# Hypermixer after linear attention on one core: k of batch 0 by token, late 64-row transposes, stores whose two tiles take tokens in turn, and another order of work

## The chip, the core and the metric

The kernel runs on one core of one Trainium2 chip. A core has five engines that run their own instruction lists and meet at semaphores: PE (matrix products and transposes, results into the eight PSUM banks), DVE (the vector engine), ACT (the scalar engine), POOL (GpSimd) and SP (SyncE, which here issues every DMA). The 16 DMA engines of the core move the data. The metric is the device time of one execution in microseconds; several executions are made, and their median is compared.

## The reference, cut to what matters

Per batch (8 of them) there are 8 heads, 576 tokens and a head size of 64. First a linear attention with cosine weights by position, then a mixing of tokens by a product of two small projections, and an output projection:

```python
r_q, r_k = relu(q), relu(k)                    # c, s: cos and sin by position
q_p = concat([r_q * c, r_q * s]);  k_p = concat([r_k * c, r_k * s])
kv  = einsum('bhsf,bhsd->bhfd', k_p, v);  z = sum(k_p, axis=2)
x   = einsum('bhsf,bhfd->bhsd', q_p, kv) / (einsum('bhsf,bhf->bhs', q_p, z) + 1e-6)
x   = x, heads side by side: (8, 576, 512)
wq, wk = x @ w_q, x @ w_k                      # 512 -> 64 each
mixed  = (wq @ wk.T / 8) @ x                   # token by token, per batch
out    = relu(mixed) @ w_out                   # 512 -> 512
```

The inputs q, k, v and the output are float32; products run in bf16 with float32 sums.

## The kernel before, in words

The unit of the first half is a group H (0 to 15) of four heads: batch H // 2, half of the heads H % 2. Each group has six loads of 288 KB (`LD.k/q/v.H.j`, two heads each, j is 0 or 1), into rings of four buffers for each of k, q and v (`N_RAW`). Where the prediction speaks of pairs, it means these groups: "pairs 6-15" are H = 6 to 15. A half group is numbered g = 2H + r.

The whole kernel is a text, `ORDER` (line 35), read word by word. `TQ.3@T0` means: step TQ for group 3 on PE, into PSUM bank 0; `@V` is DVE, `@A` ACT, `@G` POOL, `@Y` SP. Each engine executes its own words in the order of the text, without overtaking, and waits where data or a buffer is missing. So a load that waits for its buffer holds every later load and store, as they are all SP's.

The steps of the first half, by group:

- `CV` (line 215) converts v to bf16, `RK` (212) makes relu of k, `DQ` (223) relu of q.
- `VK` (218) multiplies v by the cosine and sine weights, on DVE. `KV` (231) sums k and v over the tokens on PE (36 products), `EK` (241) takes the result out of PSUM.
- `TQ` (245) transposes q on PE: 18 transposes, each on 64 rows of the array. `EQ` (254) multiplies these by the weights, on DVE.
- `NM` (264) gives numerator and denominator of a half group, `RC` (281) adds epsilon to the denominator and inverts it (lines 286 and 287), `XN` (289) multiplies, giving the rows x, on DVE.
- `XT` (300) transposes x on PE. All groups are in `XT_FULL`: ten transposes of 128 by 128. `EX` (317) copies them out of PSUM into xT.

The second half, by batch b:

- `WQK` (328) is the projection of x to q and k at once, with the features on the partitions: 64 rows of wq and 64 of wk. `EW` (337) takes it out. `DW` (341) copies the q rows down to partitions 64 to 127, since the two halves of `MX` need them there.
- `TK` (344) transposes the k rows back so that tokens lie on the partitions; `EWK` (352) takes this out. `KX` (356) sums k times x over the tokens; `EKX` (365) takes it out.
- `MX` (372) multiplies by q, `EMX` (384) applies relu and the scale, into mix.
- `WO` (399) is the output projection of one tile of 128 tokens, four products of 512 columns; `EO` (407) takes it out, `ST` (412) stores a unit of one or two tiles. Units are listed in `UNITS` and `UNITS7` (lines 29, 30); the tiles of batches 2n and 2n+1 lie together, so that nine tiles make two batches.

`LW` and `CW` load and convert the weights. Everything around a word's place in its engine's list, and its PSUM bank, is written out by hand in `ORDER`.

Of the kernel before, what the change touches and what calls it, by code (L numbers as in the profile page):

```python
# [21 lines left out]
EPS = 1.0e-6  # L22
EPS_HI = 9.9837780e-07

N_RAW, N_RK, N_VB, N_VV, N_QD, N_QPT, N_KV = 4, 2, 2, 3, 3, 4, 3
N_XS, N_XT, N_WQK, N_WKJ, N_KX, N_MIX, N_OSB = 3, 2, 2, 2, 2, 2, 8
EPS_PE = False
XT_FULL = (0, 1, 2, 3, 4, 5, 6, 7, 8, 9, 10, 11, 12, 13, 14, 15)
# [7 lines left out]
LD.v.0.1@Y LD.q.1.0@Y LD.v.1.0@Y LD.v.0.0@Y LD.v.1.1@Y LD.k.0.0@Y LD.q.1.1@Y LD.q.0.0@Y  # L36
LD.q.0.1@Y DQ.1.0@A LD.k.0.1@Y CV.0.1@A LD.k.2.1@Y CV.0.0@A LD.k.1.0@Y VK.0.0@V CV.1.1@A
LD.k.1.1@Y VK.0.1@V LD.v.3.0@Y VK.1.1@V DQ.1.1@A LD.q.2.0@Y DQ.0.0@G LD.q.2.1@Y TQ.1@T0 EQ.2@V
RK.0.0@G DQ.0.1@A LD.q.3.0@Y CV.1.0@A LD.v.2.0@Y RK.0.1@G TQ.0@T2 EQ.0@V LD.q.3.1@Y KV.0@T4
EQ.1@V LD.v.2.1@Y EK.0@A EQ.3@V NM.0@T2 LD.k.2.0@Y RK.1.1@A VK.1.0@V NM.1@T4 RK.1.0@A RC.1@V  # L40
LD.k.3.1@Y XN.1@V KV.1@T0 DQ.2.0@G LW.qk@Y RC.0@V EK.1@A CV.3.0@G XN.0@V LD.v.3.1@Y NM.2@T0
RK.2.1@G NM.3@T4 DQ.3.0@A LD.q.5.0@Y RC.2@V XT.0@T2 VK.3.0@V LD.k.3.0@Y CV.2.0@G RC.3@V XN.2@V
DQ.3.1@A LD.q.5.1@Y DQ.2.1@G XN.3@V EX.0@A LD.k.4.0@Y TQ.3@T0 TQ.2@T6 VK.2.0@V XT.1@T4
LD.q.4.0@Y CV.2.1@A EQ.4@V RK.2.0@G EX.1@A LD.v.4.0@Y VK.2.1@V LD.q.4.1@Y CW.qk@G EQ.6@V KV.2@T2
RK.3.1@G EQ.5@V CV.3.1@A LD.v.4.1@Y WQK.0@T4 EK.2@A VK.3.1@V LD.v.5.1@Y NM.5@T2 EW.0@A EQ.7@V
NM.4@T6 LD.k.4.1@Y RK.3.0@G RC.4@V TK.0@T5 DW.0@G RC.5@V LD.k.5.0@Y EWK.0@A KV.3@T0 XN.5@V
DQ.5.1@A KX.0@T5 LD.v.5.0@Y RK.4.0@G EK.3@A XN.4@V EKX.0@A NM.7@T0 DQ.4.0@G LD.k.5.1@Y NM.6@T2
RC.7@V MX.0.2@T4 RC.6@V XT.2@T6 CV.4.0@G LW.o@Y EMX.0.2@A XN.7@V EX.2@A DQ.4.1@G LD.v.6.0@Y
XN.6@V DQ.5.0@G LD.k.6.0@Y TQ.4@T0 CV.4.1@A MX.0.3@T2 EQ.8@V XT.3@T4 CV.5.1@G LD.q.6.0@Y TQ.5@T6
EQ.9@V EX.3@A LD.k.6.1@Y VK.4.0@V MX.0.1@T0 LD.q.6.1@Y RK.4.1@A VK.4.1@V WQK.1@T4 EMX.0.1@A  # L50
LD.v.6.1@Y CV.5.0@G EQ.10@V EMX.0.3@A KV.4@T0 RK.5.0@G LD.q.7.0@Y EW.1@A VK.5.0@V EK.4@A TK.1@T5
RK.5.1@A VK.5.1@V NM.9@T0 MX.0.0@T2 EWK.1@A RC.9@V EMX.0.0@A KV.5@T4 XN.9@V CW.o.0@G LD.v.7.1@Y
KX.1@T3 EK.5@A EQ.11@V CW.o.1@A NM.10@T0 LD.v.7.0@Y CV.6.0@G NM.11@T4 RC.10@V LD.q.8.0@Y
RK.6.0@A WO.0.3@T2 XN.10@V DW.1@G EKX.1@A LD.k.7.1@Y DQ.6.0@A RC.11@V MX.1.0@T0 NM.8@T6 XN.11@V
EO.0.3@A LD.q.7.1@Y RK.6.1@G WO.0.0@T3 EMX.1.0@A VK.6.0@V LD.k.7.0@Y DQ.6.1@A MX.1.1@T4
MX.1.3@T0 RC.8@V WO.0.1@T2 EO.0.0@A CV.6.1@G LD.v.8.0@Y XN.8@V EMX.1.1@A WO.0.2@T3 LD.v.8.1@Y
VK.6.1@V EMX.1.3@A EO.0.1@A MX.1.2@T4 CV.7.1@G LD.q.8.1@Y TQ.6@T0 EO.0.2@A KV.6@T6 EQ.12@V
CV.7.0@G LD.k.8.0@Y EMX.1.2@A XT.5@T2 EQ.13@V EK.6@A LD.q.9.1@Y XT.4@T4 DQ.7.0@A VK.7.0@V
WO.1.4@T7 EX.5@A LD.k.8.1@Y VK.7.1@V NM.12@T0 LD.v.9.1@Y DQ.7.1@G EX.4@A WO.1.0@T6 RC.12@V
LD.q.10.1@Y RK.7.0@G XN.12@V NM.13@T2 EO.1.4@A RK.7.1@G LD.v.9.0@Y TQ.7@T4 EO.1.0@A RC.13@V  # L60
WQK.2@T0 DQ.8.0@G EQ.15@V LD.v.10.0@Y XN.13@V CV.8.1@G KV.7@T6 EW.2@A LD.q.9.0@Y CV.8.0@G
EQ.14@V DQ.8.1@A WO.1.3@T3 LD.q.10.0@Y VK.8.1@V EK.7@A TQ.8@T0 LD.k.9.1@Y EO.1.3@A VK.8.0@V
NM.15@T4 RK.8.0@A WO.1.1@T2 EQ.16@V LD.k.9.0@Y RK.8.1@G DQ.9.1@A EQ.17@V TK.2@T3 NM.14@T6
EO.1.1@A RC.15@V EWK.2@A KV.8@T0 RC.14@V DQ.10.1@G XN.15@V WO.1.2@T3 EK.8@A CV.9.1@G DW.2@A
XN.14@V XT.6@T0 CV.9.0@G EO.1.2@A VK.9.1@V NM.16@T4 LD.v.13.0@Y EX.6@A KX.2@T7 LD.k.10.0@Y
VK.9.0@V LD.k.10.1@Y XT.7@T2 DQ.9.0@G RC.16@V EKX.2@A LD.v.10.1@Y XN.16@V NM.17@T0 EX.7@A
RK.9.1@G LD.v.11.0@Y TQ.9@T6 RC.17@V LD.q.11.0@Y MX.2.2@T4 RK.9.0@G XN.17@V LD.q.11.1@Y
EMX.2.2@A MX.2.0@T2 DQ.10.0@G LD.v.11.1@Y EMX.2.0@A EQ.19@V MX.2.1@T0 ST.1.1@Y KV.9@T4 EMX.2.1@A
EQ.18@V RK.10.0@G LD.k.11.0@Y TQ.10@T2 EK.9@A MX.2.3@T0 LD.k.11.1@Y RK.10.1@G EQ.21@V WQK.3@T6
EMX.2.3@A CV.10.0@G EQ.20@V CV.10.1@A XT.8@T0 EW.3@A VK.10.0@V NM.18@T2 EX.8@A NM.19@T4  # L70
VK.10.1@V TK.3@T7 WO.2.1@T6 DW.3@G RC.19@V RC.18@V DQ.11.1@A XN.19@V WO.2.3@T1 DQ.11.0@G
CV.11.0@A XN.18@V CV.11.1@G EO.2.1@A KV.10@T4 LD.v.15.0@Y VK.11.0@V LD.q.12.0@Y XT.9@T2 EK.10@A
EWK.3@A LD.q.12.1@Y VK.11.1@V NM.20@T4 EX.9@A ST.0.1@Y TQ.11@T6 RK.11.0@G RC.20@V KX.3@T0
LD.q.13.1@Y XN.20@V EO.2.3@A RK.11.1@G LD.v.12.0@Y WQK.4@T2 EQ.22@V EKX.3@A LD.v.12.1@Y
LD.k.12.1@Y EQ.23@V KV.11@T0 EW.4@A LD.v.13.1@Y DQ.12.0@G NM.21@T4 LD.k.12.0@Y EK.11@A MX.3.1@T2
CV.13.0@G TK.4@T7 RC.21@V ST.1.0@Y MX.3.0@T0 EMX.3.1@A WO.2.2@T6 XN.21@V DQ.12.1@G EMX.3.0@A
DW.4@G MX.3.2@T2 EWK.4@A LD.q.13.0@Y TQ.12@T4 EMX.3.2@A NM.23@T0 EQ.24@V KX.4@T7 EO.2.2@A
DQ.13.1@G LD.k.13.1@Y EQ.25@V MX.3.3@T2 EKX.4@A CV.12.0@G ST.0.0@Y WO.2.0@T6 EMX.3.3@A RC.23@V
CV.12.1@A LD.k.13.0@Y VK.12.0@V MX.4.2@T4 NM.22@T2 EO.2.0@A XN.23@V WO.3.0@T7 LD.q.15.1@Y
RK.12.1@G EMX.4.2@A RC.22@V XT.10@T0 LD.v.14.1@Y VK.12.1@V EO.3.0@A WO.3.4@T6 EX.10@A XN.22@V  # L80
LD.q.14.1@Y RK.12.0@G MX.4.1@T4 VK.13.0@V LD.q.14.0@Y KV.12@T2 EO.3.4@A CV.15.0@G LD.k.14.1@Y
XT.11@T0 EMX.4.1@A WO.3.2@T7 EK.12@A DQ.13.0@G EX.11@V LD.v.14.0@Y CV.13.1@A RK.13.1@A NM.25@T2
VK.13.1@V MX.4.0@T0 TQ.13@T4 LD.k.14.0@Y EMX.4.0@A WO.3.1@T6 EQ.26@V EO.3.2@A LD.k.15.0@Y
# [21 lines left out]
def kernel(  # L105
# [28 lines left out]
    def ring(name, shape, dtype, n):  # L134
# [333 lines left out]
    for t in qpt:  # L468
        V.memset(t[:, :, 0, :], 0.0)
# [34 lines left out]
```

## Time and profile before

| quantity | value |
|---|---|
| median of 10 runs | 123.41 us (122.1 to 125.08) |
| the profiled execution | 122.7 us, of which the span is 120.9 |
| mean granted PE clock | 0.958 |
| data by DMA | 39.38 MB, mean 326 GB/s over the span |
| last product of PE ends, last copy by ACT begins | 117.23, 117.26 us |
| loads of 288 KB, from issue to landing | 5.9 to 6.0 us in the median |
| paired stores of 512 KB (15), single stores of 256 KB (6) | 4.7 and 2.5 us to landing |

The page gives for each engine the time that it was busy, then the span in 40 slices of 3 us: a digit is the busy share in tenths, PEclk the granted clock of PE in tenths, DMA the busy share of the DMA engines. A product on PE is recorded with its whole way through the array (a product of 512 columns as 379 ns), while the next one starts long before it is out; how fast PE works when it has no gaps is better read from a run of many. The chain of waits goes back from the last instruction to what released it, and so on to the start; its pieces in order of time tell which engine set the pace in which stretch.

### The profile page before, as it was taken

The page shows a single profiled execution, that of the slowest core. Times are in us where ns is not written, and L with a number is a line of the kernel's source. Part 1 is how long each engine was busy: PE and PEld are TensorE (multiplying, and loading weights), DVE is VectorE, ACT ScalarE, POOL GpSimd, SP SyncE. Part 2 cuts the span into 40 slices and gives each one's busy share as a digit, 9 for nine tenths or more (in the row PEclk, how much of TensorE's full clock was granted, in tenths as well). Part 3 has the DMA queues.
Part 4 walks back from the last instruction along what each step waited for, and adds up shares of the span by engine and source line. Part 5 has one row for each costly group of instructions (what it writes and reads, how often), then busy time and mean ns, then how long its engine had stood idle before and what let it go on. Part 6 is the DMA issues. An engine that isn't in the chain of part 4 may idle for free.

```text
span 120.9 us, 4895 instructions
## 1 busy us (share of the span) xinstructions
PE 101.8 (84%) x2056; PEld 65.1 (54%) x2070; DVE 86.7 (72%) x174; ACT 91.8 (76%) x155; POOL 56.7 (47%) x90
## 2 busy tenths in 40 slices
PE   5902865699777999998979999999999999999970
PEld 1302754467645537655847576455746765653420
DVE  2035989948999988999999997988899489412000
ACT  7846538445897999786999789998879763988870
POOL 6505084449649459869433955534484320020000
PEclk9999599657999999999999999999999999999999
DMA  3999999999999999995999499999998796244595
GB/s 98 322 378 401 400 393 326 383 393 395 383 398 383 387 389 387 387 365 157 345 322 375 123 325 392 357 406 409 399 407 323 286 377 229 93 178 180 215 346 214
DMA packets 20374, 39.38 MB, mean 326 GB/s; under 512 B 2944, under 2 KB 2944, under 8 KB 20352
## 3 DMA queue, kind: packets, MB, share of 16 engines
q1 hardware_dynamic: 20352, 39.07, 88.9%
q8 instruction: 16, 0.26, 0.9%
q14 instruction: 6, 0.05, 0.1%
HBM read 29.62 MB, written 9.44 MB: 323 GB/s over the span
## 4 chain that ended last, share of the span: by engine, by line
DMA 40%; PE 38%; DVE 9%; issue 3%; SPq 3%; ACT 2%; POOL 1%; POOLq 0%
DMA qf<-in_q_dram 20%; PE banks L403 17%; DMA vf<-in_v_dram 11%; DMA kf<-in_k_dram 9%; PE banks L271 4%; PE banks L332 4%; PE banks L236 3%; PE banks L379 3%; DVE xs L292 3%; PE banks L310 3%; SPq L197 3%; PE banks L360 3%; DVE vv L219 3%; DVE qpt L257 2%; POOL rk L190 1%
## 5 line engine op out<-in xcount | busy, mean ns | idle before, releaser
L403 PE MATMUL banks<-wo_sb,mix 128*128 128x512 bf16 x130 | 33.6, 380 | 1.4 <-issue 1.0
L219 DVE TENSOR_TENSOR vv<-vb,cossin 128x1152 bf16<-128x1152 bf16 x32 | 27.2, 876 | 6.9 <-ACT vb L180 6.7
L292 DVE TENSOR_TENSOR xs<-banks,rec 128x640 bf16<-128x640 f32 x32 | 25.2, 809 | 0.5
L257 DVE TENSOR_TENSOR qpt<-banks,cst 128x1152 bf16<-128x1152 bf16 x32 | 22.9, 747 | 3.5 <-PE banks L250 3.2
L190 POOL TENSOR_SCALAR rk<-kf 128x576 bf16<-128x576 f32 x25 | 17.7, 713 | 10.6 <-DMA kf<-in_k_dram 7.8
L180 ACT COPY osb<-banks 128x512 f32<-128x512 f32 x36 | 20.8, 593 | 2.2 <-PE banks L403 1.7
L391 ACT ACTIVATE mix<-banks 128x576 bf16<-128x576 f32 x31 | 19.6, 661 | 2.5 <-PE banks L379 1.4
L190 POOL TENSOR_SCALAR qd<-qf 128x576 bf16<-128x576 f32 x18 | 13.6, 758 | 14.3 <-DMA qf<-in_q_dram 13.9
L403 PEld LDWEIGHTS <-mix 128*128 128x128 bf16 x144 | 12.2, 98 | 13.2 <-issue 1.1
L184 POOL TENSOR_SCALAR vb<-vf 128x576 bf16<-128x576 f32 x20 | 15.6, 786 | 5.1 <-DMA vf<-in_v_dram 2.7
L180 ACT COPY xT<-banks 128x1280 bf16<-128x1280 bf16 x13 | 15.9, 1228 | 0.9 <-PE banks L310 0.9
L271 PE MATMUL banks<-kvs,qpt 64*128 64x65 bf16 x640 | 15.3, 196 | 1.0 <-ACT kvs L180 1.0
L236 PE MATMUL banks<-vv,rk 64*64 64x131 bf16 x576 | 14.1, 237 | 2.1 <-POOL rk L190 0.8
L271 PEld LDWEIGHTS <-qpt 64*128 64x128 bf16 x640 | 12.9, 98 | 4.7 <-issue 3.0
L236 PEld LDWEIGHTS <-rk 64*64 64x64 bf16 x576 | 10.7, 116 | 5.3 <-issue 2.0
L250 PE MATMUL banks<-ident,qd 64*128 64x64 bf16 x288 | 7.0, 192 | 6.6 <-ACT qd L188 4.9
L184 POOL TENSOR_SCALAR wq<-wqk 64x576 bf16<-64x576 bf16 x7 | 4.7, 667 | 16.5 <-ACT wqk L180 15.6
L188 ACT ACTIVATE qd<-qf 128x576 bf16<-128x576 f32 x14 | 9.6, 687 | 3.1 <-DMA qf<-in_q_dram 3.1
L310 PE MATMUL banks<-ident,xs 128*128 128x128 bf16 x160 | 11.3, 219 | 0.7 <-DVE xs L292 0.7
L310 PEld LDWEIGHTS <-xs 128*128 128x128 bf16 x160 | 9.5, 98 | 3.0 <-DVE xs L292 1.0
L332 PE MATMUL banks<-xT,wqk_sb 128*128 128x288 bf16 x64 | 10.1, 306 | 0.8 <-ACT xT L180 0.7
L180 ACT CAST kvs<-banks 128x262 bf16<-128x262 f32 x16 | 6.1, 383 | 5.7 <-PE banks L236 5.4
(42 smaller groups left out, 104.3 us busy)
## 6 DMA issues: line engine op xcount, KB each, us to landing
vf<-in_v_dram SPq DMA_DIRECT2D x32, 288.0 KB, 5.9
qf<-in_q_dram SPq DMA_DIRECT2D x32, 288.0 KB, 6.0
kf<-in_k_dram SPq DMA_DIRECT2D x32, 288.0 KB, 5.9
out_dram<-osb SPq DMA_DIRECT2D x15, 512.0 KB, 4.7
out_dram<-osb SPq DMA_DIRECT2D x6, 256.0 KB, 2.5
wo_f<-in_moe_w_out_dram SPq DMA_DIRECT2D x1, 1024.0 KB, 7.9
w_f<-in_moe_w_q_dram SPq DMA_DIRECT2D x1, 128.0 KB, 7.3
w_f<-in_moe_w_k_dram SPq DMA_DIRECT2D x1, 128.0 KB, 7.1
```

Source lines behind the costliest of these rows:

```text
L180: A.copy(dst, src)
L184: eng.tensor_scalar(dst, src, 1.0, 1.0, op0=ALU.mult, op1=ALU.mult)
L190: eng.tensor_scalar(dst, src, FMAX, 0.0, op0=ALU.min, op1=ALU.max)
L219: eng.tensor_mul(vv[H % N_VV][:, j, :, :, 0:D], vb[H % N_VB][:, j].unsqueeze(2).to_broadcast([P, C9, 2, D]), cossin)
L236: T.matmul(kvp[64 * j:64 * j + 64, r, :], rk[H % N_RK][64 * r:64 * r + 64, j, c, :], vv[H % N_VV][64 * r:64 * r + 64, j, c].rearrange("p w ...
L257: eng.tensor_mul(qpt[g % N_QPT][:, :, 1:SLOTS, :], qt.unsqueeze(1).to_broadcast([P, 2, C9, D]), cst)
L271: T.matmul(nv[:, j, u, :], qpt[g % N_QPT][p0:p0 + 64, w, 2 * u:2 * u + 2, :], kvs[H % N_KV][p0:p0 + 64, r, w, 0:D + 1], start=(u == 0 and ...
L292: eng.tensor_tensor(xs[b % N_XS][:, :, 4 * h + r:4 * h + r + 3:2, :].rearrange("p u h d -> p h u d"), num_view(at["NM", g])[:, :, :, 0:D], ...
L310: T.transpose(xv[:, i, u, :], x, ident)
L332: T.matmul(w[:, nh, :], wqk_sb[:, dmc, :], xT[b % N_XT][:, dmc, D + nh * HS:D + (nh + 1) * HS], start=(dmc == 0), stop=(dmc == NDM - 1))
L391: A.activation(dst, src, AF.Relu, scale=scale_moe)
L403: T.matmul(o, mix[b // 2 % N_MIX][:, dmc, base:base + P], wo_sb[:, dmc, :], start=(dmc == 0), stop=(dmc == NDM - 1))
```

## The change

There are six parts.

1. `XT_FULL` holds only groups 0 to 5. Groups 6 to 15 take the other branch of `XT`, which was there before and was not used: 20 transposes of 64 rows by 128, half of them into each of two banks; `EX` then copies in runs of 64 elements.
2. `WK_DIRECT = (0,)`: for batch 0 a new step `WK` computes k of the hypermixer with the tokens on the partitions at once. `WQK` of batch 0 uses weights with w_q twice, so that both halves of `MX` find their q rows; `TK.0` and `DW.0` are gone. A new weight conversion `CW.qq` is added. `EX.0` and `EX.1` come in two halves each.
3. `EPS_PE` is now the list (0, 1, 2, 3): for these groups epsilon is added by two small products at the end of `NM`, and `RC` only inverts. Their constants are made by POOL at the start.
4. `IN_TURN`: in a unit of two tiles, tile t takes every second token. The weights of `WO` are read with a step of two, and one partition holds two neighbouring rows of the output, so that `ST` writes 4 KB at once instead of twice 2 KB.
5. The rings `qpt` and `rec` have the same size as before and another shape. The steps `EQm`, `NMm`, `RCm`, `XNm` are defined and not used.
6. `ORDER` is another text. The loads begin with all six of group 0, then those of group 1. By engine: CV 12 on ACT and 20 on POOL become 5 and 27; RK 7 and 25 become 9 and 23; the three EWK of DVE (batches 5, 6, 7) go to ACT; of `EX`, DVE had groups 11, 13 and 14 and has 4, 13 and 15. `CW.qk` is on ACT instead of POOL.

```diff
-EPS_PE = False
-XT_FULL = (0, 1, 2, 3, 4, 5, 6, 7, 8, 9, 10, 11, 12, 13, 14, 15)
+EPS_PE = (0, 1, 2, 3)
+XT_FULL = (0, 1, 2, 3, 4, 5)
+WK_DIRECT = (0,)
+IN_TURN = True
...
-LD.v.0.1@Y LD.q.1.0@Y LD.v.1.0@Y LD.v.0.0@Y LD.v.1.1@Y LD.k.0.0@Y LD.q.1.1@Y LD.q.0.0@Y
-LD.q.0.1@Y DQ.1.0@A LD.k.0.1@Y CV.0.1@A LD.k.2.1@Y CV.0.0@A LD.k.1.0@Y VK.0.0@V CV.1.1@A
...
+LD.k.0.0@Y LD.q.0.0@Y LD.q.0.1@Y LD.v.0.0@Y LD.v.0.1@Y LD.k.0.1@Y LD.v.1.0@Y LD.q.1.0@Y
+LD.v.1.1@Y RK.0.0@G DQ.0.0@A LD.q.1.1@Y DQ.0.1@G LD.k.1.1@Y TQ.0@T0 CV.0.0@G LD.k.1.0@Y CV.0.1@A
+LD.v.2.0@Y VK.0.0@V VK.0.1@V LD.v.2.1@Y RK.0.1@A EQ.1@V CV.1.0@G LD.q.2.1@Y KV.0@T2 LD.q.2.0@Y
+VK.1.0@V EK.0@A EQ.0@V CV.1.1@G LD.k.2.1@Y DQ.1.0@A NM.1@T2 DQ.1.1@A LD.k.2.0@Y VK.1.1@V NM.0@T0
+RC.1@V LD.q.3.0@Y RK.1.1@G TQ.1@T4 RC.0@V XN.1@V LD.q.3.1@Y RK.1.0@A XN.0@V CV.2.0@G LW.qk@Y
+KV.1@T2 EQ.3@V CV.2.1@G LD.v.3.0@Y EQ.2@V XT.0@T0 EK.1@A DQ.2.1@G LD.v.3.1@Y NM.2@T2 VK.2.0@V
...
+VK.15.1@V NM.28@T4 EW.6@A MX.5.0@T0 WO.3.3@T7 RC.28@V EMX.5.0@A DW.6@G XN.28@V RK.15.1@A
+MX.5.1@T2 TK.6@T6 NM.29@T0 EWK.6@A KV.15@T4 RC.29@V EMX.5.1@A XN.29@V KX.6@T6 EK.15@A NM.31@T2
+EKX.6@A NM.30@T0 EO.3.3@A RC.31@V MX.6.1@T4 WO.5.4@T6 RC.30@V EMX.6.1@A ST.3.2@Y XN.31@V
+WO.5.0@T7 EO.5.4@A XN.30@V MX.6.0@T2 EO.5.0@A XT.14@T4 XT.15@T0 EX.14@A ST.5.0@Y WO.5.3@T6
...
 def WQK(eng, pb, b):
     w = bank2(pb, 0, 4 * HS, FP32)
+    wq = wqq_sb.rearrange("p c w j -> p c (w j)") if b in WK_DIRECT else wqk_sb
...
+def WK(eng, pb, b):
+    o = bank1(pb, 0, 4 * SC * DH, FP32)
+    for u in range(SC):
+        for dmc in range(NDM):
+            T.matmul(o[:, u * DH:(u + 1) * DH], xT[b % N_XT][:, dmc, u * P:(u + 1) * P],
+                     wqk_sb[:, dmc, DH:2 * DH], start=(u == 0 and dmc == 0),
+                     stop=(u == SC - 1 and dmc == NDM - 1))
...
 def WO(eng, pb, b, t):
-    base = (t + 4 * (b % 2)) * P
+    n, ts = unit_of[b, t]
+    k = len(ts) if IN_TURN else 1
+    base = ((ts[0] + 4 * (b % 2)) * P + ts.index(t) if IN_TURN else (t + 4 * (b % 2)) * P)
     for dmc in range(NDM):
-        T.matmul(o, mix[b // 2 % N_MIX][:, dmc, base:base + P], wo_sb[:, dmc, :],
-                 start=(dmc == 0), stop=(dmc == NDM - 1))
+        T.matmul(o, mix[b // 2 % N_MIX][:, dmc, base:base + k * (P - 1) + 1:k],
+                 wo_sb[:, dmc, :], start=(dmc == 0), stop=(dmc == NDM - 1))
...
 def ST(eng, pb, b, u):
+    if IN_TURN:
+        ap = [[k * DM, P], [1, k * DM]]
+        src = src.rearrange("p t n -> p (t n)")
```

The words of `ORDER` that the prediction leans on, SP's list after, from the middle on: ... LD.q.8.1 LD.k.8.1 LD.q.11.1 LD.v.9.1 LD.k.9.1 LD.q.9.0 LD.q.9.1 LD.k.10.1 LD.q.12.1 LD.v.10.0 LD.v.10.1 LD.q.10.0 LD.k.10.0 ST.1.0 LD.q.10.1 LD.q.11.0 LD.k.11.0 LD.k.11.1 LD.v.11.0 LD.v.11.1 LD.q.14.0 ST.0.1 LD.v.12.1 LD.v.12.0 LD.q.12.0 LD.q.13.1 LD.v.15.0 LD.v.13.0 ... LD.q.15.0 ST.2.1 ST.1.2 LD.k.15.1 LD.k.15.0 ST.2.0 ST.4.0, and then only stores.

PE's list begins, after: TQ.0 KV.0 NM.1 NM.0 TQ.1 KV.1 XT.0 NM.2 NM.3 TQ.2 KV.2 XT.1 NM.4 NM.5 TQ.3 WK.0 WQK.0 KX.0 KV.3; before: TQ.1 TQ.0 KV.0 NM.0 NM.1 KV.1 NM.2 NM.3 XT.0 TQ.3 TQ.2 XT.1 KV.2 WQK.0 NM.5 NM.4 TK.0 KV.3 KX.0.

## The prediction

> **What bounds the kernel now.** Views were read in this order: the page's head, its chain, the chain piece by piece, the three-microsecond windows, the timelines of the vector engine (DVE) and of SP, and the groups. No engine alone is the bound:
>
> ```profile
> span 120.9 us, 4895 instructions
> PE 101.8 (84%) x2056; PEld 65.1 (54%) x2070; DVE 86.7 (72%) x174; ACT 91.8 (76%) x155; POOL 56.7 (47%) x90
> ...
> PEclk9999599657999999999999999999999999999999
> DMA  3999999999999999995999499999998796244595
> ```
>
> The chain, followed piece by piece, has three stretches: loads until 53.45 us, mostly DVE from 54.6 to 61 (and DVE mixed with ACT until 67.9), and PE alone from 67.88 to the last eviction at 117.26. The last stretch holds pieces like these (start, length, what):
>
> ```profile
> 96.61 0.26 PE banks L250 x18
> ...
> 103.00 1.12 PE banks L310 x20
> ...
> 111.93 4.64 PE banks L403 x21
> ```
>
> They give PE's pace when it is full: 18 small transposes of q in 0.26 us (14 ns each, 64-row tiles in pairs), 20 full transposes in 1.12 us (56 ns each), a matmul of the output product in 221 ns.
>
> The loads do not set the end although their queue is 89% busy. SP stopped twice, at 50.9-55.2 and 62.1-67.4 us:
>
> ```profile
> 49.96 0.96 SPq L197 DMA_DIRECT2D kf<-in_k_dram  x2
> 55.21 0.33 SPq L197 DMA_DIRECT2D vf<-in_v_dram  x1
> ...
> 60.41 1.66 SPq L197 DMA_DIRECT2D kf<-in_k_dram  x2
> 67.42 0.33 SPq L197 DMA_DIRECT2D vf<-in_v_dram  x1
> ```
>
> By the order these are LD.v.13.0 (behind CV.9.0) and LD.v.15.0 (behind CV.11.0): loads hoisted before their buffer is free. DMA ran dry for some 2 us each time, yet in those windows DVE stayed at 2.9 of 3 us. So DVE, ACT and PE hold the middle, PE the end.
>
> **The change, part by part**, against the profiled execution: 122.7 us, a span of 120.9 and 1.8 around it.
>
> *The start.* The groups show what DVE waited for first: ACT's vb, 6.1 us, until 7.87. Load number n landed at about 4.2 + 0.74 n us: the timeline has number 4 used at 7.17, 7 at 9.31, 8 at 10.13, 9 at 10.81, each after a wait for that DMA. Before, the first loads are a mixture of pairs 0 and 1; after, pair 0 comes whole. I walk DVE through the new order with 0.75 for VK and EQ, 0.81 for XN, 0.22 for a reciprocal, 0.67 for a conversion. v.0.0 (number 4) at 7.2, CV.0.0 to 7.9, VK.0.0 and VK.0.1 to 9.4, EQ.1 to 10.1, VK.1.0 (load 7) to 10.9, EQ.0 to 11.6, VK.1.1 (load 9) to 12.4, two reciprocals 12.8, XN.1 and XN.0 to 14.5, EQ.3 and EQ.2 to 16.0, VK.2.0 and VK.2.1 to 17.5, reciprocals, XN.3 and XN.2 to 19.5. PE is in time: k.1.0 is load 12 (13.1), RK 0.69, KV.1 0.72, EK 0.38: 14.9. Before, the four XN of pairs 0 and 1 end at 20.65 with one VK fewer done. The lead is 1.15 + 0.75 = **1.9 us**, four epsilon additions included. It is kept, since DVE is busy 2.8 to 3.0 of 3 us in all windows but one from 30 to 72.
>
> *Epsilon on PE for pairs 0-3.* Eight additions (L286, 151 ns) go; four are in the walk, four give **0.6**. PE gets 16 tiny matmuls, at 21 ns (twenty of L271 in 0.42 us) 0.3 us, where it idles a quarter of the time: nothing.
>
> *k of batch 0 by token.* Five transposes, DW.0 (POOL 0.67) and the wait of TK for EW leave; 20 matmuls with full 128x128 weights come: 20 x 56 ns = 1.1 us by the full transposes, 2.2 where the clock is at half. Two conversions of weights (CW.qk on ACT, CW.qq on POOL) replace one, and EX.0, EX.1 come in halves (two more fixed parts on ACT, about 0.4 us). From XT.1 to KX.0 the old chain took 7.15 us (21.46 to 28.61). The new one is at most 1.5 (EX.1) + 0.6 + 2.2 + 2.1 (WQK.0 as measured, at half clock) = 6.4. That path is not DVE's; what DVE gains is that NM.4 and NM.5 stand before WK.0 and WQK.0. The trace has 1.27 us of idle DVE at 26.0-27.3 behind WQK.0. But KV.3 and NM.6 now stand behind both. Ends 0 and 1.3; I take **0.6**.
>
> *64-row transposes for pairs 6-15.* Ten full ones (0.56 us) become twenty on 64 rows. The nearest row is L250, the same tile (64x128 weights, 64 moving): 20 x 14.4 = 0.29 us, a saving of 0.27 a pair. Against it stands the Trainium skill, "TensorEngine Tiling (Array Packing)", Instruction Overhead: a matmul carries some 60 cycles, so that a free size of 1 costs as much as 60, and one should not take the tiling factor from a dimension that is already small. This change takes it from exactly that one, the moving 128 becomes 64. By the page 20 x 25 ns (estimate from its 60 cycles at 2.4 GHz) = 0.50, a saving of 0.06. The row decides, being the same instruction on the same tile. Pairs 6-9 fall before 68 us, where PE is not last: nothing. Pairs 10-15: 6 x 0.27 = **1.6** (0.4 by the page). The copy EX then reads and writes runs of 64. On ACT, the strided EMX took 661 ns where the plain EW took 641 for as many elements: 20 ns, nothing. On DVE (EX.13, EX.15) no row has this form; between the 0.82 measured and XN's rate (809 ns for 640 elements: 1.6 us), nearer to EQ, which also reads bf16 banks at 0.65 ns an element: 0.82.
>
> *Tokens in turn.* WO's weights step by two elements in 30 of 36 products. The load (98 ns) hides under a matmul of 221; even doubled it does. No row has a stepped load; gain excluded, a load of four times 98 would cost 171 ns x 120. The Trainium skill, "TensorE: Matmul & The Clock Gate", Weight-path perf modes, keeps the fast load for steps up to 1,024 elements; no run here shows it. Taken: 0. The 15 paired stores, 7.86 MB, move 4 KB packets. The last 2 KB stores ran at about 380 GB/s, the 2.25 KB loads at about 400: at 405 it is 20.7 - 19.4 = 1.3 us of DMA time, hidden by PE's stretch. No loss from half the packets. The last stores of batch 7 that end the run are single tiles, unchanged.
>
> *Engines.* EX.4 comes onto DVE at about 45 us, where DVE is short: **+0.8**; EX.11 leaves it at 82, where it waited for PE: 0. The three EWK (325 ns) leave DVE for ACT late, where DVE had waits of up to 2.8 us: 0; ACT pays 3 x 0.44. Seven CV go from ACT to POOL, two RK the other way: POOL +3.4 us, ACT about 1 less net. VK takes 876 ns on average and about 750 where POOL rests, 4.0 us for POOL's 56.7 busy; 3.4 more are **+0.2** on DVE. After the last XN PE has 12 WO instead of 11, one MX fewer (0.23) and cheaper transposes already counted: +0.6, but WO work earlier is less by as much: 0.
>
> Sum: -1.9 - 0.6 - 0.6 - 1.6 + 0.8 + 0.2 = -3.7. For waits that a new order brings and no row can show I leave 0.5: **-3.2**, 119.5 for the profiled execution. The median before lies 0.7 above that execution, so the forecast is **120.2 us**.
>
> **Rivals.**
> *The gain is used up on the way* (within 0.5%, about what a measurement of this kernel can tell from no change): ACT is at 2.8-3.0 us of 3 in half the windows from 39 to 93. If its order stalls EK or EX, the lead of 1.9 + 1.2 ends in DVE idling and the page's price for the transposes leaves 0.4: 123.0. For it: full ACT. Against: ACT has about 1 us less to do.
> *SP stops too long* (slower). The new order hoists four loads: q.11.1 (behind DQ.7.1), q.12.1 (DQ.8.1), q.14.0 (DQ.10.0) and v.15.0 (CV.11.0), and v.9.1 and all of pair 10 stand behind the first two. Landing takes 5.9 us. Before, the last load landed at 93.8 and 27.1 us followed. After KV.15 the new order has 14 WO (12.6), two KX (1.3), two NM (0.8), seven MX (1.6), two XT (0.6), WQK, TK (1.1): 18, with RK.15, KV.15 and the last store 23 us. It decides from a last load (k.15.0) later than 94.7 us. Each stop left DMA dry for 2 us before; four stops of 3 give 12 instead of 4, a landing at about 101.8 and a median of 101.8 + 23 + 1.8 + 0.7 = 127; two harmful ones about 125. For it: the two stops in the old trace. Against: 7 stores, not 6, stand before the last load but the queue had over 5 us of slack, and 4 KB packets help.
> *More than forecast*: the lead of the start also removes the half-clock stretch (slices at 5, 6, 5, 7 between 12 and 30 us cost PE about 4.9 us); half of it back gives 117.7.
>
> **How the numbers follow.** Forecast 0.58 (its own range 118.6 to 122.3), more 0.09, no change 0.09, slower 0.24 (SP's stops 0.18; stepped weights or the DVE copy 0.06). Faster 0.67, same 0.09, slower 0.24. The range, 117.3 to 125.3, cuts a third of the "more" case and half of the slower one.
>
> **What would show it.** XN of pair 1 done near 19.5 us; L310's successor at 64x128 in about 0.3 us a pair; WO still about 221 ns a matmul; stores of 4 KB packets above 400 GB/s and no shorter end for it; DVE's epsilon rows x24. Wrong if the last k load lands after 94.7, if DVE idles over 8 us between 30 and 100, or if WO's pace leaves 221 ns.

## The result, and the profile after

| quantity | before | after |
|---|---|---|
| median, measured side by side | 123.58 us (121.21 to 126.06, 41 runs) | 125.22 us (123.68 to 127.57, 12 runs) |
| ratio after to before | | 1.019, 95% interval 1.0137 to 1.0244 |
| profiled execution, its span | 122.7, 120.9 us | 125.66, 123.8 us |
| last XN done, and from there to the end of the span | 103.3, 17.6 us | 103.4, 20.4 us |

The change makes the kernel slower by about 1.6 us. The forecast was 120.2. (A ratio compares undisturbed executions alone; it need not be the quotient of two medians.)

The head of the page after; its rows are busy time, granted clock and DMA share, as before:

```profile
span 123.8 us, 5153 instructions
PE 101.2 (82%) x2181; PEld 63.7 (51%) x2201; DVE 83.7 (68%) x161; ACT 90.5 (73%) x156; POOL 60.1 (49%) x100
...
PEclk9998595589999999999999999999999999999999
DMA  4999999999999998599999999964999945544095
```

PE, DVE and ACT have all become a little less busy while the span grew by 2.9 us: the change did take work away, and waits took its place. Where the waits are, the view of waits says ("waited for: us in total, times, longest us"). First before, then after, the rows between the mix evictions (EMX, on ACT) and the output products (WO, on PE):

```profile
ACT mix L391 <- PE banks L379: 1.4, 3, 0.5
```

```profile
ACT mix L452 <- PE banks L467: 5.5, 6, 1.4
PEld L467 <- ACT mix L452: 2.7, 3, 1.1
PE banks L467 <- ACT mix L452: 1.8, 3, 1.0
```

L467 is WO, L452 is EMX on ACT, L454 the one EMX on DVE (EMX.7.0). Before, EMX waited only for its own products MX (L379). After, it waits six times for **WO**, and WO for it. An eviction into mix has no reason to wait for a product that reads other tokens of mix. In the last stretch of the chain of waits (start, length, what), which was PE alone before, the two now take turns:

```profile
108.43 0.98 PE banks L467 x4
109.44 1.20 ACT mix L452 x2
110.69 0.82 PE banks L467 x3
...
112.65 0.66 ACT mix L452
...
113.55 0.77 DVE mix L454
114.36 0.83 PE banks L467 x3
115.22 0.66 ACT mix L452
115.93 4.29 PE banks L467 x19
```

Before, this stretch had 21 products in one piece of 4.64 us and no eviction of mix among the last pieces.

Which steps these are can be read from the wait lists of the compiled programs. Added by the change, each absent before:

```
EMX.1.3 <- WO.0.0    EMX.1.2 <- WO.0.1    EMX.3.3 <- WO.2.0    EMX.5.2 <- WO.4.0
EMX.6.3 <- WO.6.1    EMX.7.1, EMX.7.2 <- WO.6.2    EMX.7.3 <- WO.6.3
WO.0.2  <- EMX.1.0   WO.2.1  <- EMX.2.3
WO.6.0  <- EMX.6.2   WO.6.3  <- EMX.7.0, EMX.7.1
```

EMX.1.3 writes tokens of batch 1, WO.0.0 reads tokens of batch 0: they share no element. The same holds for every pair of the list: with the addresses of the compiled programs taken element by element, each pair shares none. WO now reads every second token of two tiles; EMX writes two blocks of mix at once. Where such a read meets such a write, the program puts in a wait. A tile of a pair in turn does need all tokens of its pair, so it can have to wait for both halves of a batch; but in the new order those evictions stand in front of it anyway.

### The profile page after: what moved, and what is told of

It is laid out like the page before. It is cut to its first block, busy times and chain, and to the rows that moved or that the text cites. A ratio compares the mean times of both kernels' runs of the same rounds, so it can differ in the third digit from the quotient of the medians.

```text
span 123.8 us, 5153 instructions
## 1 busy us (share of the span) xinstructions
PE 101.2 (82%) x2181; PEld 63.7 (51%) x2201; DVE 83.7 (68%) x161; ACT 90.5 (73%) x156; POOL 60.1 (49%) x100
## 4 chain that ended last, share of the span: by engine, by line
PE 48%; DMA 16%; ACT 12%; issue 8%; DVE 7%; SPq 3%; POOL 3%; POOLq 0%; ACTq 0%
PE banks L467 22%; DMA qf<-in_q_dram 10%; PE banks L252 6%; ACT mix L452 6%; DMA kf<-in_k_dram 6%; PE banks L293 4%; PE banks L382 3%; SPq L206 3%; PE banks L440 3%; PE banks L266 3%; PE banks L421 3%; DVE xs L323 2%; DVE vv L233 2%; PE banks L360 2%; PE banks L356 2%
## 5 line engine op out<-in xcount | busy, mean ns | idle before, releaser
L467 PE MATMUL banks<-wo_sb,mix 128*128 128x512 bf16 x124 | 34.2, 381 | 3.8 <-ACT mix L452 1.8
L189 POOL TENSOR_SCALAR vb<-vf 128x576 bf16<-128x576 f32 x27 | 20.0, 743 | 14.7 <-DMA vf<-in_v_dram 10.0
L323 DVE TENSOR_TENSOR xs<-banks,rec 128x640 bf16<-128x640 f32 x32 | 24.4, 798 | 0.1
L452 ACT ACTIVATE mix<-banks 128x576 bf16<-128x576 f32 x31 | 19.7, 655 | 6.3 <-PE banks L467 5.5
L195 POOL TENSOR_SCALAR rk<-kf 128x576 bf16<-128x576 f32 x23 | 17.1, 747 | 9.3 <-DMA kf<-in_k_dram 5.0
L467 PEld LDWEIGHTS <-mix 128*128 128x128 bf16 x144 | 12.1, 98 | 16.1 <-ACT mix L452 2.7
L252 PE MATMUL banks<-vv,rk 64*64 64x131 bf16 x576 | 13.5, 232 | 4.4 <-DVE vv L233 1.5
L185 ACT COPY xT<-banks 128x1280 bf16<-128x1280 bf16 (+1 forms) x15 | 16.1, 1091 | 0.9 <-PE banks L356 0.7
L293 PE MATMUL banks<-kvs,qpt 64*128 64x65 bf16 x640 | 14.8, 194 | 1.1 <-ACT kvs L185 0.5
L293 PEld LDWEIGHTS <-qpt 64*128 64x128 bf16 x640 | 12.6, 96 | 4.7 <-issue 2.5
L266 PE MATMUL banks<-ident,qd 64*128 64x64 bf16 x288 | 7.8, 196 | 4.8 <-POOL qd L195 2.2
L266 PEld LDWEIGHTS <-qd 64*128 64x128 bf16 x288 | 6.0, 98 | 8.7 <-issue 4.2
L440 PE MATMUL banks<-wqk,kx 64*128 64x288 bf16 x36 | 8.6, 287 | 0.9 <-ACT mix L452 0.3
L382 PE MATMUL banks<-xT,wqk_sb 128*128 128x288 bf16 x56 | 8.1, 287 | 0.4 <-ACT xT L185 0.4
```

The source lines that it names most:

```text
L185: A.copy(dst, src)
L189: eng.tensor_scalar(dst, src, 1.0, 1.0, op0=ALU.mult, op1=ALU.mult)
L195: eng.tensor_scalar(dst, src, FMAX, 0.0, op0=ALU.min, op1=ALU.max)
L252: T.matmul(kvp[64 * j:64 * j + 64, r, :], rk[H % N_RK][64 * r:64 * r + 64, j, c, :], vv[H % N_VV][64 * r:64 * r + 64, j, c].rearrange("p w ...
L266: T.transpose(qt[:, r, c * D:(c + 1) * D], qd[H % N_QD][p0:p0 + 64, c, :, :], ident[p0:p0 + 64, p0:p0 + 64])
L293: T.matmul(nv[:, off + step * j, u, :], qpt[H % N_QPT][p0:p0 + 64, r, w, 2 * u:2 * u + 2, :], kvs[H % N_KV][p0:p0 + 64, r, w, 0:D + 1], st ...
```

## The experiments

Theory A: these mutual waits are what the change lost by. Theory B: SP's stops, the rival that the prediction had. The expectations of the first kernels call it theory C that the stepped loads or the packets themselves are slow; further down, theory C is another one, of PE's code. Every row of this table is one kernel; "XN" is the end of the last XN in its profile, "tail" the time from there to the end of the span. The profile is one execution; the ratio is the judge.

| kernel | median us | ratio to before, 95% interval | XN | tail |
|---|---|---|---|---|
| before | 123.41 | | 103.3 | 17.6 |
| after | 125.22 | 1.019 (1.0137 to 1.0244) | 103.4 | 20.4 |
| after, tiles apart | 121.31 | 0.9805 (0.9712 to 0.9898) | 101.3 | 18.7 |
| before, in turn | 127.6 | 1.0356 (1.0287 to 1.0425) | 106.9 | 19.5 |
| after, in turn, mix laid out anew | 121.9 | 0.9806 (0.971 to 0.9902) | 103.5 | 18.7 |
| after, ST.3.0 late | 125.61 | 1.0146 (1.0055 to 1.0237) | 104.0 | 20.4 |
| after, in turn for batches 0 to 5 | 123.56 | 0.9937 (0.9881 to 0.9994) | 103.6 | 18.8 |
| after, in turn for batches 6 and 7 | 123.17 | none; before had 122.76 | 100.7 | 20.4 |

### Tokens in turn taken out of after, and put into before

```diff
 # after, tiles apart
-IN_TURN = True
+IN_TURN = False
```

> The changed kernel with IN_TURN off: its order of work, its transposes, its k of batch 0, but every tile of a store has 128 tokens in a row again, weights of WO unstepped, 2 KB packets. Theory A (WO reading mix with a step makes EMX wait for WO and WO for EMX, where their tokens do not meet; the last 12 us become a relay of PE and ACT): 2.5 to 4 us faster than the changed kernel, so a ratio to the kernel before of 0.985 to 1.000, and ACT's mix no longer waits for WO (5.5 us in the changed kernel). Theory B (SP stands at ST.3.0 in front of the last seven loads, so they land late): no change, ratio 1.015 to 1.025. Theory C (the stepped weight loads or the packets themselves are slow): also faster, but with the same waits named in the trace.

```diff
 # before, in turn (and, so that no wait closes a circle, one word moved)
+IN_TURN = True
...
-... MX.6.1@T0 TK.7@T6 WO.6.3@T3 EMX.6.1@A ...
+... MX.6.1@T0 TK.7@T6 EMX.6.1@A WO.6.3@T3 ...
```

with `WO` and `ST` as in the change.

> The kernel before with IN_TURN alone, and WO.6.3 put behind EMX.6.1 in the text, which it now needs. Theory A: EMX.1.0, 1.1, 1.3, 3.0, 3.3, 5.1, 7.2 and 7.3 now wait for a WO, and WO.6.1 for EMX.7.0 and 7.1; ratio 1.015 to 1.03, the loss in the last 15 us. Theory B: 1.00 (SP's list is unchanged). Theory C: slower, with WO at more than 221 ns a product.

Measured: 0.9805 and 1.0356. The one edit is worth 3.8 points in the new order and 3.6 in the old. The waits go and come with it. After with the tiles apart, all that is left of the kind:

```profile
ACT mix L452 <- PE banks L440: 2.4, 4, 1.2
```

Before with tokens in turn:

```profile
ACT mix L390 <- PE banks L404: 5.3, 8, 0.9
PEld L404 <- ACT mix L390: 3.6, 7, 1.0
```

In the first, EMX waits for its own products (L440 is MX there); in the second for WO (L404), as in the changed kernel. (Here one new wait is real: WO.6.3, in turn, shares tokens with EMX.6.1, and for this the word was moved.) The chain of the first still has one short turn of ACT and DVE at the end (1.11 and 0.77 us of EMX from 109.5 to 111.7), so its tail is 18.7 us and not the 17.6 of before. Without tokens in turn the other five parts of the change are a gain of 2.0%, not far from the 2.6% that the forecast saw in the whole.

### Step, packets or waits

Tokens in turn does three things: it steps PE's weights, it makes 4 KB packets, and it brings the waits. This kernel keeps the first two and loses the third: mix is laid out so that the evictions of one half lie apart from those of the other.

```diff
-mix = ring("mix", [P, NDM, 2 * S], BF16, N_MIX)
+mix = ring("mix", [P, 2, 2 * S, 2], BF16, N_MIX)
...
-        dst = mix[b // 2 % N_MIX].rearrange("p (r i) n -> p r i n", r=2)[
-            :, :, i, o:o + NT].rearrange("p r (d c) -> p r d c", c=C9)
+        dst = mix[b // 2 % N_MIX][:, i, o:o + NT, :].rearrange("p (d c) r -> p r d c", c=C9)
...
-        T.matmul(o, mix[b // 2 % N_MIX][:, dmc, base:base + k * (P - 1) + 1:k], ...
+        T.matmul(o, mix[b // 2 % N_MIX][:, dmc % 2, base:base + k * (P - 1) + 1:k, dmc // 2], ...
```

> The changed kernel, still with tokens in turn and 4 KB packets, but mix is laid out as [half of the features, token, other half], so that what one EMX writes is one closed block and WO steps by 4 (2 where a unit has one tile) inside it; the waits of EMX for WO and of WO for the wrong EMX are gone from the program. Theory A: as fast as e1, ratio 0.985 to 1.000. Theory C: 1.02 or more, since the step is larger, and WO takes more than 221 ns a product. Theory B: 1.015 to 1.025. If ACT pays for writing every second element, EMX is longer than 655 ns.

Measured 0.9806: the same as with the tiles apart, with all stores of pairs still in 4 KB packets and the weights stepped even wider. In its compiled program no EMX waits for a WO, and WO waits for the same EMX as with the tiles apart. Its groups (busy us, mean ns of one):

```profile
L466 PEld LDWEIGHTS <-mix 128*128 128x128 bf16 x144 | 14.0, 114 | 12.7 <-issue 0.8 <-DVE mix L453 0.7
```

against the changed kernel's

```profile
L467 PEld LDWEIGHTS <-mix 128*128 128x128 bf16 x144 | 12.1, 98 | 16.1 <-ACT mix L452 2.7 <-issue 0.8 <-DVE mix L454 0.7
```

A step of two loads as fast as no step did before (98 ns both). The 114 ns are a mean: the 120 loads of tiles in pairs, with a step of four, took some 117, the other 24, with a step of two, 98. EMX, which writes every second element here, takes 827 ns in place of 655, 5.3 us more of ACT in 31 of them, and still the time is the same. So the step, the packets and ACT's work are not what the change lost by; the waits are.

### SP's stop in front of the last loads

SP's timeline after (start, us, what it issues):

```profile
77.03 0.33 SPq L206 DMA_DIRECT2D qf<-in_q_dram  x1
83.27 0.34 SPq L487 DMA_DIRECT2D out_dram<-osb  x1
83.67 1.54 SPq L206 DMA_DIRECT2D vf<-in_v_dram  x1
...
88.10 2.19 SPq L206 DMA_DIRECT2D kf<-in_k_dram  x2
```

SP stands from 77.4 to 83.3 behind ST.3.0, which waits for its tile, with seven loads behind it; the last k load goes out at 89 to 90 and lands at about 97, past the 94.7 from which the prediction's rival was to decide. Two kernels put that store behind the loads:

```diff
 # in after: ST.3.0 taken from in front of LD.v.14.0 and put
+LD.k.15.0@Y ST.3.0@Y
 # in after with tiles apart: the same store put
+LD.q.15.0@Y ST.3.0@Y
```

> The changed kernel with the word ST.3.0 behind LD.k.15.0 instead of in front of the last seven loads. Theory B: the loads land some 5 us earlier, the gap of DMA at 81 to 87 us goes, ratio 0.995 to 1.008. Theory A: the relay at the end stays, ratio 1.012 to 1.02.

> e1 with ST.3.0 behind LD.q.15.0 instead of in front of LD.v.14.0: SP no longer stands from 75.4 to 81.0 us. If late loads hold the end in e1 (PE idles half of 90 to 93 us, behind DQ.15.0): 1 to 2 us faster, ratio 0.965 to 0.975. If PE catches up by its backlog of WO: as e1, 0.978 to 0.983.

The first gave 1.0146 (1.0055 to 1.0237), which does not differ from the 1.019 of after. The second had a median of 121.93 (118.11 to 123.56, no interval) where 121.31 stood without the move. SP's stop is there, as the rival said, but taking it away brings nothing that can be seen. The kernel with mix laid out anew says the same from the other side: SP stands there from 78.6 to 83.8, its last load lands at 97 too, and it is at 0.9806.

### Where in the run the waits cost

```diff
 # in turn for batches 0 to 5
-IN_TURN = True
+IN_TURN = (0, 1, 2, 3, 4, 5)
...
-        k = len(ts) if IN_TURN else 1
+        k = len(ts) if b in IN_TURN else 1
 # and in a second kernel
+IN_TURN = (6, 7)
```

> The changed kernel, tokens in turn for batches 0 to 5, apart for 6 and 7 (their stores in 2 KB packets). Left of the mutual waits between evictions of mix and output products: evictions 1.2, 1.3, 3.3 and 5.2 behind WO of the batch before. Theory A1 (the relay in the tail is most of the loss): 0.98 to 0.995 of the kernel before, with the last stretch of WO on PE unbroken as in the kernel with all tiles apart. Theory A2 (the early waits are what costs, by ACT standing still in the middle): 1.01 or more, as the changed kernel.

> The complement of the run with tokens in turn for batches 0 to 5: here only batches 6 and 7 are in turn. Waits of evictions of mix on output products: 6.3, 7.1, 7.2, 7.3; none before the tail. If the loss splits by place and adds up, the tail is worth what that run won against the changed kernel (1.019 to 0.994, about 0.025) on top of the kernel with all tiles apart (0.98 to 0.985): 1.005 to 1.01. If the tail's relay is nearly all of it: 1.015 to 1.02. If the early waits matter only where the late ones follow (the two overlap): near 1.019 as well; if either alone is hidden: 0.98 to 0.99.

Measured 0.9937 (0.9881 to 0.9994), and medians of 123.17 against 122.76 of before, 1.003, without an interval. From 0.9805 the early waits cost 1.3 points and the late ones about 2.3; the two together should give 1.0165, and after has 1.019. So both places seem to count, and neither is nearly all. The late part is the surer one: 0.9937 is clear of 1.019. The early part is not clear of noise, as the intervals of 0.9805 and 0.9937 just overlap. The tail shows the late part cleanly. With batches 6 and 7 in turn it is 20.4 us in all three kernels that have it so, and the chain of the second kernel is after's, piece by piece:

```profile
105.69 0.98 PE banks L467 x4
106.70 1.20 ACT mix L452 x2
107.95 0.82 PE banks L467 x3
...
109.91 0.66 ACT mix L452
110.81 0.77 DVE mix L454
111.63 0.84 PE banks L467 x3
112.48 0.66 ACT mix L452
113.19 4.29 PE banks L467 x19
```

With them apart it is 18.7 or 18.8 in the table. So 1.7 us of the late loss are seen in the tail. The early loss (EMX.1.2, 1.3, 3.3 and 5.2) should show in the XN column: 103.4 and 103.6 with those waits, 101.3 and 100.7 without. But the kernel with the new layout has 103.5 without them, so a single profile is no proof of that column; the ratios are.

### The other parts one by one

The first two of these kernels stand on before, the others on after with tiles apart, so that the waits don't mask them:

```diff
 # before, 64-row transposes for groups 6 to 15
+XT_FULL = (0, 1, 2, 3, 4, 5)
 # before, 64-row transposes for groups 10 to 15 alone
+XT_FULL = (0, 1, 2, 3, 4, 5, 6, 7, 8, 9)
 # after with tiles apart, full transposes in all groups
+XT_FULL = (0, 1, 2, 3, 4, 5, 6, 7, 8, 9, 10, 11, 12, 13, 14, 15)
 # after with tiles apart, epsilon on DVE everywhere
+EPS_PE = ()
 # after with tiles apart, EX.0.1 put directly behind EX.0.0
+EX.0.0@A EX.0.1@A
```

> The kernel before with XT_FULL = (0, ..., 5) alone: pairs 6 to 15 are transposed in 64-row tiles, the order is the old one. If the step of the prediction holds (0.27 us of PE a pair, six of them where PE is last): 1.6 us faster, ratio 0.985 to 0.990. If the small transposes cost what the page on tiling says: 0.4 us, ratio 0.996 to 1.000. If PE was not last there after all (the engines are balanced and DVE or ACT takes over): 0.995 to 1.003 although PE's work is shorter.

> The kernel before, x of the pairs 10 to 15 alone in 64-row tiles. With pairs 6 to 15 it was 1.03. If the loss comes from what pairs 6 to 9 move in the middle (SP's long stop at a hoisted load, 62 to 68 us, and the granted clock there), it is gone: 0.985 to 1.0, the gain of the late pairs standing alone. If the 64-row form itself costs (clock, or the copy reading runs of 64), 1.015 to 1.03.

> The changed kernel with all tiles apart and x transposed whole in all 16 pairs: in the new order the 64-row tiles alone are undone. By the prediction's step (0.27 us of PE in each of six late pairs) it is 1.6 us slower than with the 64-row tiles apart: ratio to the kernel before about 0.994. If the 64-row tiles cost time of themselves, as they did in the old order (1.03), it is faster than 0.98; if they are off the path, equal to 0.98.

> e1 with EPS_PE empty: epsilon of pairs 0 to 3 is added on DVE again. The prediction gave 0.6 us to four of the additions and counted four more in the start: up to 1.2 us slower than e1, ratio 0.985 to 0.990. If DVE's wait at 20 to 22 us swallows them: as e1, 0.978 to 0.983.

> e1 (the changed kernel with the tiles apart) with EX.0.1 moved directly behind EX.0.0 in ACT's list, in front of EK.2, which waits for KV.2. The bank of XT.0 then comes free earlier, NM.5 and RC.5 start earlier, and most of the 2.1 us that DVE sits idle before 22.4 us should go. If the early lead carries to the end: 1 to 2 us faster than e1, ratio 0.965 to 0.975. If DVE is not what sets the end later on, the same as e1, 0.978 to 0.983.

| kernel | median us | ratio to before, 95% interval |
|---|---|---|
| before, 64-row for groups 6 to 15 | 125.37 | 1.0295 (1.0183 to 1.0406) |
| before, 64-row for groups 10 to 15 | 123.44 | 1.0006 (0.9966 to 1.0046) |
| after apart, full transposes | 121.97 | 0.9895 (0.9844 to 0.9946) |
| after apart, epsilon on DVE | 126.44 | 1.0245 (1.0033 to 1.0456) |
| after apart, EX.0.1 early | 121.67 | 0.9864 (0.9799 to 0.993) |

The last is no gain over 0.9805. But it did not do what it was made for. DVE's wait in front of the inversions of group 2 (L305, L303 in the other kernel), without and then with EX.0.1 moved:

```profile
22.44 0.29 DVE L305 RECIPROCAL rec<-banks 128x10 f32<-128x10 f32 x2 [2.15 <-ACT xT L185]
23.45 0.29 DVE L303 RECIPROCAL rec<-banks 128x10 f32<-128x10 f32 x2 [2.59 <-ACT xT L183]
```

The wait is still there, so it was not the bank that EX.0.1 frees. In the kernel with EX.0.1 moved, PE waits 0.75 us for POOL's relu of k, starts KV.2 at 19.70, and goes on without a gap, at a granted clock of 0.50, through XT.1, NM.4 and NM.5 to 23.3. What this wait costs is not shown.

Undoing the 64-row tiles in the new order costs 0.9 points with intervals that overlap: their part is some 1 us, where 1.6 were counted, and may be none. In the old order the six late groups gave nothing, and all ten lost 3%, which nobody had expected. And moving eight small additions back to DVE lost 4.4 points where 1.2 us were counted. Edits this small do not move this much work. The timeline of PE in the kernel with epsilon on DVE shows something else (idle time before the group stands in brackets, with what ended it):

```profile
76.85 0.36 PE L360 MATMUL banks<-ident,xs 64*128 64x64 bf16 x14
80.14 0.26 PE L360 MATMUL banks<-ident,xs 64*128 64x64 bf16 x6 [2.92 <-issue]
```

One step's 20 transposes, all with the same data ready: after 14 of them PE stands for 2.92 us and waits for nothing that the trace knows.

### Stops of PE that belong to no wait

Such stops were looked for in all traces: "issue" behind a group of matmuls, over 0.25 us. Before has none. The 16 others have 48 between them. To each the number of PE's records (matmuls and weight loads) from the start up to it was counted, out of the view by windows, and taken modulo 256: **all 48 lie between 174 and 191**. Kernels with quite different orders stop at the same counts. The page's rows on DMA queues fit to that. Before, then after:

```profile
q8 instruction: 16, 0.26, 0.9%
```

```profile
q8 instruction: 17, 0.28, 0.9%
```

Sixteen packets for 4,126 records of PE, seventeen for 4,382: about 258 each. Theory C: a packet is a block of PE's code, and PE stands where its next block is late.

The traces keep every packet's own time, and these times bear it out. Each packet of q8 has 16,384 bytes. Three of the stops (the kernel of the last row is explained below):

| kernel | packet, from and to, us | PE stands, us | from the packet's end to PE |
|---|---|---|---|
| after apart | 66.64, 67.54 | 67.84 to 69.06 | 1.52 |
| after apart, epsilon on DVE | 77.73, 78.68 | 77.22 to 80.14 | 1.46 |
| after apart, 64 more instructions | 69.02, 69.90 | 69.27 to 71.31 | 1.41 |

It is so in all: **each of the 48 stops ends 1.2 to 1.6 us after the end of such a packet**. The next packet starts only after the stop, when PE has gone into the new block: in 46 cases, with the DMA engines busy for 0.98 or more of the time until then, 2.0 to 5.3 us after; in the two with them busy for under 0.1, 1.1 us. So with full DMA engines the next block comes later.

Three kernels put more PE instructions ahead of the work, in the time of the warming matmuls at the start:

```diff
-    for _ in range(N_WARM):
+    for _ in range(10):
         T.matmul(bank1(7, 0, 2048, FP32), warm[:, 0:P], warm, start=True, stop=True)
+    for _ in range(36):
+        T.matmul(bank1(7, 0, 256, FP32), warm[:, 0:P], warm[:, 0:64], start=True, stop=True)
```

(64 more instructions; with 6 and 72 in their place 128 more), in the kernel after with tiles apart and in before with 64-row tiles for groups 6 to 15.

> The changed kernel with all tiles apart, and 64 more PE instructions ahead of the work: 4 of the 14 warming matmuls (8 records with their weight loads) give way to 36 small ones (72 records), in about the same time. Theory C: PE stands still where a block of 256 of its instructions is not there yet. Counted in PE's records (matmuls and weight loads) from the start, all stops of over 0.25 us that nothing in the profile explains lay at 256 n + 175 to 192 in every trace so far; they stay at these counts here, and so fall on work 64 records earlier (the one in KX.2 at 69 us is no longer there). Ratio within 0.97 to 1.0, by how many blocks come late. If the stops belong to the work and not to the count (a semaphore that the trace does not show), the one in KX.2 stays and the counts become 256 n + 240 to 256.

> The kernel before with x of pairs 6 to 15 in 64-row tiles (1.0295 as it stood) and the same 64 PE instructions ahead. By theory C the loss of that kernel was stops at its blocks (2.4 us of them after 90 us, where PE is last, 1.4 us before); with the boundaries moved against the work the stops fall elsewhere: the time follows the sum of the stops seen in its profile, with 1.00 if that sum is under 1 us and 1.03 again if it is about 4. If the 64-row form or the copy of it is what costs, 1.03 without regard to the stops.

> As the kernel with 64, with 128 PE instructions more (8 warming matmuls give way to 72 small ones). By theory C the stops stay at 256 n + 175 to 192 of PE's records, and the time follows their sum and whether they lie after 90 us; between 0.99 and 1.03. If the 64-row form itself costs, 1.03.

| kernel | ratio to before, 95% interval | stops over 0.25 us, us | of that after 90 us |
|---|---|---|---|
| after apart | 0.9805 (0.9712 to 0.9898) | 2.9 | 0 |
| the same, 64 more | 0.9891 (0.9829 to 0.9954), median 124.05 against 123.32 | 5.3 | 0 |
| after apart, epsilon on DVE | 1.0245 (1.0033 to 1.0456) | 6.7 | 0.3 |
| before, 64-row for 6 to 15 | 1.0295 (1.0183 to 1.0406) | 4.1 | 2.4 |
| the same, 64 more | 1.0059 (1.0018 to 1.0099) | 4.4 | 0 |
| the same, 128 more | 1.0103 (1.0058 to 1.0149) | 1.6 | 0 |

Where the stops lie is as theory C said. In after with tiles apart one fell into KX.2 (L421), after its first product of ten:

```profile
67.54 0.30 PE L421 MATMUL banks<-xs,wkj 128*64 128x256 bf16 x1
69.06 0.71 PE L421 MATMUL banks<-xs,wkj 128*64 128x256 bf16 x9 [1.23 <-issue]
```

With 64 instructions more ahead, that one is gone, and PE stops earlier in its list, within the products of NM (L293), at a count of 185 modulo 256:

```profile
71.31 0.28 PE L293 MATMUL banks<-kvs,qpt 64*128 64x65 bf16 x7 [2.04 <-issue]
71.42 0.58 PE L360 MATMUL banks<-ident,xs 64*128 64x64 bf16 x20
```

A stop that belongs to the work would have moved with the work. (The small products also change the warming a little; what that does by itself was not tried.) What theory C said of the time came out only in part. Most of the 3% of the old order with 64-row tiles is not the tiles but goes with the place of the code: with the same tiles and moved code it is 0.6 or 1.0%. But the time does not follow the sum of the stops: 4.4 us of them went with 1.0059 and 1.6 us with 1.0103. The kernel at 1.0295 is the one with stops after 90 us, where PE sets the end. And one execution's stops are not another's: the same stop in KX.2 was 1.2 to 2.6 us long in seven traces and 0.24 in an eighth.

The stops are no rival to theory A. The kernels that decide on it have about as much of them: after 2.6 us, the same with tiles apart 2.9, with mix laid out anew 2.5; before none, before in turn 0.6.

## Why the prediction was wrong

Step by step, as it stood.

- **Tokens in turn, "Taken: 0". This step failed.** It asked what the stepped load costs PE, and what the packets bring DMA, and both answers were right: 98 ns a load as before; 4 KB packets at 406 GB/s where 2 KB ones ran at 375, 1.1 us less of DMA's time (107.5 us, then 106.4; counted 1.3), and no shorter end for it. It did not ask what the new reads of mix do to the waits around them. They cost 3.8 points (1.019 against 0.9805), some 4.7 us, more than the whole of the forecast gain. No rival named them either: "slower" stood for SP's stops, stepped weights or the copy on DVE. The change adds no work for it, and no row of the trace before shows it; but that a read with a step spans what it doesn't touch was in the diff.
- The start, -1.9: right. XN of group 1 is done at 18.7 (forecast 19.5, before 20.65). It was to be kept, "since DVE is busy"; it was not. Twelve XN are done at 40.6 against 44.4 before, 24 at 73.8 against 74.2, the last at 103.4 against 103.3: a lead that even grew was lost between 41 and 74 us. From 30 to 100 us DVE is idle for 10.2 us (6.8 before), so the sign "over 8" came true; but it is 9.9 in the faster kernel with tiles apart, which keeps 2 us of the lead (24 XN at 72.0, the last at 101.3). DVE also stands 2.90 us before 22.93; what that costs was not shown, since moving EX.0.1 did not remove it.
- Epsilon on PE, -0.6 beside the start's: the additions did go (x24 left), but undoing it cost 5.1 us in the median (126.44 against 121.31), not 1.2. The profile of that kernel has 3.8 us more of PE's stops, which with 1.2 makes 5.0; that the stops are the cause was not tried by itself.
- k of batch 0 by token, -0.6: not tried by itself. The path it speaks of became shorter than counted: from XT.1 to KX.0 it takes 4.5 us (21.57 to 26.05), where it took 7.15 and 6.4 were the most.
- 64-row transposes, -1.6: the price of one was right. The chain after has, for two groups,

```profile
103.68 0.58 PE banks L360 x40
```

  which is 0.29 us for 20: the row of the trace was right, and not the 0.50, the estimate from the 60 cycles of the Trainium skill's "TensorEngine Tiling (Array Packing)", Instruction Overhead. The gain was mis-sized: 0 in the old order for the six late groups (1.0006), 0.9 points at best guess in the new, not clear of noise.
- EX.4 on DVE, +0.8, and the 64-row copies there: the three EX of DVE take 821 ns on average, as taken. POOL +3.4 us: 60.1 against 56.7, exact; VK goes from 876 to 882 ns, 0.2 us in 32, as counted.
- WO after the last XN, "+0.6, but 0": the tail of after with tiles apart is 18.7 against 17.6 before, so 1.1. (The forecast also counted one MX fewer after the last XN; the lists have seven both times, so it is one WO more, some 0.9. Behind KV.15 the list after has eight MX, not seven.)
- "PE alone from 67.88": nearly; the chain before has POOL and a stand that it doesn't explain from 77.56 to 80.48. No term rests on it.
- "For waits that a new order brings and no row can show", 0.5: the right place, a tenth of the size.

Of the rivals, SP's stops did come as described (last load at about 97, over its limit of 94.7), and the result fell on their side, yet they were not why: two kernels without the long one are no faster. Without tokens in turn the forecast would have stood: 121.31, in its own range of 118.6 to 122.3. That would have been luck in part, since the pieces of the sum did not come at their sizes. The 0.9805 makes that kernel, and the one with mix laid out anew (0.9806), faster than both kernels of the change.

What stays open: whether the early waits really cost their 1.3 points, and how (ACT standing, or what stands behind it); and how much of each small edit's time is code that comes late.

## What to carry to other kernels

When a change alters how a tile is read or written, list the waits of the compiled program before and after and look at every pair that is new: a read with a step against a write in blocks may be taken for an overlap that isn't one, and no instruction in the diff tells of it. It can be had without the waits by laying the tile out so that what is written together is read together. And in a kernel with thousands of small PE instructions do not trust the sign of a one-line edit to less than about 2% unless the place of the code has been moved too: here that place went with a change of one kernel from 1.0295 to 1.0059.

## What the hardware showed that was not expected

PE stops between blocks of 256 of its instructions when the next block is not there: 48 stops of 0.26 to 2.92 us in 16 traces, all at a count of 174 to 191 modulo 256 of the recorded ones (instructions that are not recorded, before the first of them, would explain that it isn't 0), and all ending 1.2 to 1.6 us after the end of a 16,384-byte packet on the queue q8. The Trainium skill, "Runtime: NRT & Kernel Launch", Instruction fetch mechanics, has blocks of 256 instructions that are fetched while the one before runs; the packets agree with that. It calls the cost of a boundary mostly hidden, which these traces do not bear out. That a block comes late because loads fill the same DMA engines is what the packets' times suggest (2.0 to 5.3 us to the next packet with the engines full, 1.1 with them empty); no run with fewer loads tried it.

After such a stop the granted clock can fall, which may be a part of why the time does not follow the sum of the stops. Between 30 and 115 us it is at half in nine stretches, in 8 of the 17 traces: eight of 3.4 us and one of 6.8. Each begins within 2.5 us of the end of one of the 48 stops; after the others in that time it stays at 1.00, after the one of 2.56 us too. In the kernel before with 64-row tiles for groups 6 to 15, the view by windows (busy time of PE, its weight loads, DVE, ACT and POOL; then granted clock, DMA share, GB/s) has

```profile
60.00:63.00 3.00, 1.91 (x47) 1.22 (x48) 2.12 (x3) 1.88 (x5) 1.51 (x3) 0.83 1.01 323
63.00:66.00 3.00, 3.00 (x56) 1.87 (x54) 2.38 (x4) 1.89 (x4) 0.00 (x0) 0.60 1.04 388
```

and before is at 1.00 in both windows.
